# One Trainium2 core: O normalised one head group at a time instead of two, with a new table of exp tiles

## The chip, the cores and the metric

The kernel runs on one core of one Trainium2 chip. The metric is the device time of one execution in microseconds (us). Before the change it was measured three times: 797.41, 797.54 and 798.36 us, median 797.54. One of these executions, of 797.54 us, was recorded by the profiler; every duration below is from that one.

## The reference, cut to what matters

A transformer layer whose two branches start from the same normalised input: multi-query attention (32 query heads of 16 columns, one shared K and one shared V) and a GELU feed-forward, with x (2048 x 512) added.

```python
xn = _layernorm(x)
q = (xn @ wq).reshape(B, S, 32, 16).transpose(0, 2, 1, 3)
k, v = xn @ wk, xn @ wv                       # one K and one V of 16 columns
p = softmax(einsum("bhqd,bkd->bhqk", q, k) * 16 ** -0.5)
o = einsum("bhqk,bkd->bhqd", p, v)
return x + o.transpose(0, 2, 1, 3).reshape(B, S, 512) @ wo + gelu(xn @ w1 + b1) @ w2 + b2
```

## The kernel before, in words

**Tiles and units.** The 2048 queries are cut into 4 blocks of 512 (`NTB`, `TBW`), the 32 heads into 8 groups of 4 (`NGR`, `HG`), so there are 32 (block, group) pairs, numbered `gg`. For each, the scores of 4 heads against 16 tiles of 128 keys make 64 score tiles of 128 keys x 512 queries, 2048 in all. Three consecutive tiles are one unit `u`; 683 units (`NU`) run one after another. A unit is three score matmuls (L851) into three of the eight PSUM banks. Units alternate between banks 0 to 2 and 3 to 5, so the scores of unit u+2 need unit u's banks read out.

**Who takes the exponential.** The string `DTAB` (L51) has one character for each unit. A dot: ScalarE takes all three tiles in one activation of 128x1536 (L870). A digit, 0 or 2: that tile of the unit goes to VectorE and ScalarE takes the other two in one activation of 128x1024. A VectorE tile, called a D tile here, is the sum of five scaled bf16 patterns: one read of PSUM (L887), then, for up to three D tiles together (`KB`), four further additions on the stored integers (L902). A batch is also closed at the last D tile of a group. A D tile costs five value matmuls (L891) instead of one. ScalarE's results stand in a ring of `NE` = 25 buffers `E` of 512 columns until TensorE has read them.

**Normalising O.** The value matmuls of one group add up in bank `pO`: four heads, 32 rows each, of which 16 are O and row 16 is the sum of the exponentials. When a group is complete, `o_evac` (L913) copies the bank to `Of` in f32 (L915), collects the four rows of sums in `den` by a DMA, inverts them on VectorE (L919) and writes them to a scratch row in HBM. Four DMAs then bring the group's 16-row pieces of `Of` to `OfP`, where two head groups fill 128 rows without gaps, and four DMAs broadcast the inverted sums to the same rows of `rbP`. After every second group one VectorE multiply of 128x512 (L937) turns both into `oTp` in bf16, which is the operand of the output projection (`wo_mm`, L1021). Group 30 has no partner and is multiplied in 64 rows; group 31, the last, goes through `o_norm_last` (L940), with its sums transposed by TensorE, no DMA, and a projection of its own (L1168).

**The rest.** Layer norm, its transposes, K and V come first. Q of later groups (`q_pack`, L968), the feed-forward (`h_mm`, `h_chain`, `y_mm`) and the output tiles of the block before (`out_tile`, L1036) are side work with a due unit each (`at`, `q_at`, L1065). An output tile adds the feed-forward, the four pairs of the attention output and the bias in bank 7 (`pM`), which all side matmuls share.

**What sets the order.** The kernel writes down every operation with the data it reads and writes; `Prog.schedule` (L192) then plays the program through with an assumed duration for each operation and fixes from it one order for each engine, `Prog.emit` the semaphore waits. At run time each engine works through its list in order. For a DMA the plan assumes 0.7 us of issue and 2.2 us to landing (L573); all the DMAs of this change are issued on SyncE's queue. When TensorE would be idle, the plan puts matmuls on zeros in between (L1184).

Of the kernel before, what the change touches and what calls it, by code (L numbers as in the profile page):

```python
# [6 lines left out]
ACT = mybir.ActivationFunctionType  # L7
ALU = mybir.AluOpType
AX = mybir.AxisListType

P = 128
# [24 lines left out]
EV_ALLOW = -2.0  # L36
S_WAIT = 0.1
P_WAIT = 0.0
NE_ND_KB = (25, 8, 3)
LA = 34  # L40
LB = 105
LY = 9
# [5 lines left out]
LCO = 0.0  # L48
PRO_FROM = 2.0
TBL = 1  # L50
DTAB = "...00.20.0022.00.2...202202.22..0.200220..220..0.02.222002.20...2200220.2.0.2220.0...200000..002002.2.00..200220..00.200.0000....02.220.22.0220.02...2.22200022.0.2..220..20200220.20.20.220....22.200.2222.020020...2220.222.0222.0.020......2.2..0..020202....0220.20..0022.02.0...22..2220.2020.22.20...0.020020002...0020...02.00..0002202.022....222.2222.2222.0000..222.0.0222.022.200....00000.2020.00.02.2...22202.2.22.0000.000...2.2200.22..22.20.0...2.2.2.002..020020....220.2200.002.22.000....000020.2200.22200...02202.2.2002..2022...222220..0.2222.0020..22.00002.02.222020....20222...0202..0..2...220....2000.2.0.22....2.2.2.00..2.002020...0.00.2202.02000.00...20022.02.00.202000...."  # L51
Y_ALLOW = 8.0
H_ALLOW = 5.0
YT_ALLOW = (3,3,3,3)
# [372 lines left out]
def bass_parallel_sum__grouped_kv_mqa__dense_activation_gelu__prompt_kernel(  # L427
# [18 lines left out]
    H, Dh = 32, 16  # L446
# [3 lines left out]
    TBW = 512  # L450
    NTB = S // TBW
    HG = 4
    NGR = H // HG
    NE, ND, KB = NE_ND_KB
    NPR = 5
    NV = 1 + len(SPL_K)
    KZ = SPL_K.index(0)
    GAM = 128.0 / LN2 * 0.25
    bf, f32 = dt.bfloat16, dt.float32
    i16, i32 = dt.int16, dt.int32  # L460

    with ExitStack() as es:
        def sb(shape, dtype, name):
            return es.enter_context(nc.sbuf_tensor(name, shape, dtype))
# [11 lines left out]
        wop = sb([P, NGR // 2, D], bf, "wop")  # L476
        wol = sb([P, D], bf, "wol")
# [13 lines left out]
        selL = sb([P, 4], f32, "selL")  # L491
# [31 lines left out]
        Dt = sb([P, len(SPL_K), ND, TBW], i16, "Dt")  # L523
        Of = sb([P, 2, TBW], f32, "Of")
        den = sb([P, 2, 16], f32, "den")
        OfP = sb([P, 2, TBW], f32, "OfP")
        rbP = sb([P, 2, TBW], f32, "rbP")
        rX = rbP[:, 0, :].rearrange("p (i r) -> p i r", i=4)
        rd_dram = nc.dram_tensor("rden_rows", [NTB * NGR, HG * TBW], f32).ap()
        oT = sb([P, TBW], bf, "oT")  # L530
        oTp = sb([P, NPR, TBW], bf, "oTp")

        pAll = es.enter_context(nc.psum_tensor("pAll", [P, 8 * 512], f32))

        def bank(b, n=1):
            return pAll[:, b * 512:(b + n) * 512]
# [6 lines left out]
        def B(b):  # L543
            return ("bank", b)
# [4 lines left out]
        def dve(fn, r=(), w=(), n=TBW, mode=1, allow=1.0, **kw):  # L549
            return add("dve", fn, r, w, occ=vcost(n, mode), lat=0.16, allow=allow, **kw)  # L550

        def act(fn, r=(), w=(), n=TBW, allow=0.0, **kw):
            return add("act", fn, r, w, occ=0.051 + n / 1.2e3, lat=0.22, allow=allow, **kw)

        def mm(o, l, rh, start, stop, r=(), w=(), tp=None, skip=False, occ=0.216, allow=1.5, **ak):
            kw = {}
            if tp is not None:
                kw["tile_position"] = tp
            if skip:
                kw["skip_group_check"] = True  # L560
            return add("pe", lambda e: e.matmul(o, l, rh, start=start, stop=stop, **kw), r, w, occ=occ, lat=0.23,  # L561
                       allow=allow, **ak)
# [10 lines left out]
        def dma(eng, o, i, stream, r=(), w=(), lat=2.2, allow=1.0, **kw):  # L573
            return add(eng, lambda e: e.dma_start(o, i), r, w, dma=stream, occ=0.7, lat=lat, allow=allow, **kw)
# [13 lines left out]
        def setup(fn, r=(), w=(), occ=0.25, due=0.0, **kw):  # L588
            return add("pool", fn, r, w, occ=occ, lat=0.15, due=due, **kw)
# [188 lines left out]
        for _, _, kind, a in sorted(steps, key=lambda s: s[:2]):  # L778
# [17 lines left out]
            due=0.0)  # L796
# [116 lines left out]
        def o_evac(gg):  # L913
            i = gg % 2
            dve(lambda e: e.tensor_copy(Of[:, i, :], pO), w=["O", ("Of", i)], allow=0.0)  # L915
            row = Of[16:17, i, :]
            dma("sp", den[:, i, :], bass.AP(row.tensor, row.offset, [[32 * row.ap[0][0], HG], [1, TBW]]),
                f"d_den{i}", r=[("Of", i)], w=[("den", i)])
            dve(lambda e: e.reciprocal(den[:, i, :], den[:, i, :]), r=[("den", i)], w=[("den", i)], n=120)  # L919
            dma("sp", rd_dram[gg:gg + 1, :], den[:, i, :], f"d_rd{i}", r=[("den", i)], w=[("rd", i)])  # L920
            pp, h = divmod(gg, 2)
            s, sl = pp % 2, pp % NPR
            for j in range(HG):
                r0 = 64 * h + Dh * j
                dma("sp", OfP[r0:r0 + Dh, s, :], Of[32 * j:32 * j + Dh, i, :], f"d_of{s}{h}{j}", r=[("Of", i)], w=[("OfP", s, h, j)])
            for j in range(HG):
                r0 = 64 * h + Dh * j
                src = rd_dram[gg:gg + 1, j * TBW:(j + 1) * TBW]
                dma("sp", rbP[r0:r0 + Dh, s, :], bass.AP(src.tensor, src.offset, [[0, Dh], [1, TBW]]), f"d_rb{s}{h}{j}",
                    r=[("rd", i)], w=[("rbP", s, h, j)])  # L930
            end = gg == NTB * NGR - 2
            if end:
                setup(lambda e: e.memset(oTp[64:P, sl, :], 0.0), w=[("oTp", sl)], occ=0.4)
            if h or end:
                n = 64 if end else P
                keys = [(k, s, hh, j) for k in ("OfP", "rbP") for hh in range(h + 1) for j in range(HG)]
                onorm[gg - h] = onorm[gg] = dve(lambda e: e.tensor_tensor(oTp[0:n, sl, :], OfP[0:n, s, :], rbP[0:n, s, :], ALU.mult),  # L937
                                                r=keys, w=[("oTp", sl)], allow=3.0)

        def o_norm_last(gg):  # L940
            RB1 = [[("rbP", 0, h, j) for j in range(HG)] for h in range(2)]
            for h in range(2):
                c = slice(h * 256, h * 256 + 256)
                dve(lambda e, c=c: e.tensor_copy(Of[:, 1, c], pO[:, c]), w=["O", ("Of", 1), ("Of", 2 + h)], n=256, due=0.0)
            for h in range(2):
                for i in (2 * h, 2 * h + 1):
                    mm(bank(h)[:, 4 * i:4 * i + 4], Of[:, 1, i * P:(i + 1) * P], selL[:], True, True,
                       r=[("Of", 2 + h), "selL"], w=[B(h)], occ=0.2, due=0.0)
            for h in range(2):
                dve(lambda e, h=h: e.reciprocal(rT[:, 2 * h:2 * h + 2, :],  # L950
                                                bank(h)[:, 8 * h:8 * h + 8].rearrange("p (i j) -> p i j", j=4)),
                    w=[B(h), ("rT", h)], n=100, due=0.0)
                o = rX[:, 2 * h:2 * h + 2, :].rearrange("p i (j r) -> p i j r", j=4)
                i_ = rT[:, 2 * h:2 * h + 2, :].unsqueeze(3).to_broadcast([P, 2, 4, 32])
                if h == 0:
                    dve(lambda e, o=o, i_=i_: e.tensor_copy(o, i_), r=[("rT", h)], w=[("rX", h)] + RB1[h], n=256, due=0.0)
                else:
                    act(lambda e, o=o, i_=i_: e.activation(o, i_, ACT.Copy), r=[("rT", h)], w=[("rX", h)] + RB1[h], n=256, due=0.0)
            for h in range(2):
                for i in (2 * h, 2 * h + 1):  # L960
                    add("pe", lambda e, i=i, h=h: e.transpose(bank(h)[:, 128 + (i % 2) * P:256 + (i % 2) * P], rX[:, i, :], ident_f[:]),
                        r=[("rX", h), "ident_f"], w=[B(h)], occ=0.15, lat=0.22, due=0.0)
            for h in range(2):
                c = slice(h * 256, h * 256 + 256)
                dve(lambda e, h=h, c=c: e.tensor_tensor(oT[:, c], Of[:, 1, c], bank(h)[:, 128:384], ALU.mult),
                    r=[("Of", 2 + h)], w=[B(h), ("oTl", 0) if h == 0 else ("oTl", 1)], n=256, due=0.0)

        def q_pack(tb, p, gls=(0, 1)):  # L968
            s = p % 2
# [51 lines left out]
        def wo_mm(tb, i, ps, start=False, bk=7, al=1.5):  # L1021
            for n, p in enumerate(ps):
                pp = tb * NGR // 2 + p
                hs = [h for h in range(2) if 2 * pp + h < NTB * NGR - 1]
                assert all(2 * pp + h in onorm for h in hs)
                mm4(bank(bk), oTp[:, pp % NPR, i * P:(i + 1) * P], wop[:, p, :], start and n == 0, False,
                   r=[("oTp", pp % NPR), "wop"], w=[B(bk)], allow=al)

        def b2_mm(bk=7, stop=True, al=1.5):
            mm4(bank(bk), ones, b2row[:], False, stop, r=["ones", "b2row"], w=[B(bk)], allow=al)  # L1030
# [134 lines left out]
        for i in range(4):  # L1165
            wo_mm(tb, i, range(FIN_G, NGR // 2), start=i < 3, bk=FB[i], al=WF_ALLOW)
        for i in range(4):
            mm4(bank(FB[i]), oT[:, i * P:(i + 1) * P], wol[:, :], False, True,  # L1168
               r=[("oTl", i // 2), "wol"], w=[B(FB[i])], due=0.0)
        for i in (0, 1, 3, 2):  # L1170
            ti = tb * 4 + i
            w = [(B(FB[i]), j) for j in range(4)] + ([B(FB[i])] if i < 3 else []) + [("x", ti)]
# [50 lines left out]
```

## Time and profile before

| | |
|---|---|
| time of the profiled execution | 797.54 us |
| its span, first to last instruction | 795.8 us |
| median of three runs | 797.54 us |
| ScalarE (ACT) busy | 774.0 us, 97% |
| TensorE (PE) busy, the zero matmuls among it | 767.0 us, 96% |
| VectorE (DVE) busy | 739.8 us, 93% |
| first exp starts, last exp ends | 30.0 us, 786.6 us |
| D tiles, and exps over three tiles | 439, 243 |

Span and time of the profiled execution differ by 1.7 us, which lie outside the recorded instructions. Busy time is the time in which at least one instruction of the engine runs; successive instructions of one engine overlap at their edges, so that a mean duration times the count comes out above it. The chain of waits follows the work that ended last back from the end, at each step to the instruction that released it, and its pieces do not overlap. "A <- B" in the table of waits says that A stood idle until B ended.

### The profile page before, as it was taken

How to read it: one execution, taken by the hardware profiler on the slowest of the kernel's cores; microseconds unless marked ns; L12 is line 12 of the kernel's file. 1: busy time of each engine (PE TensorE's matmuls, PEld its weight loads, DVE VectorE, ACT ScalarE, POOL GpSimd, SP SyncE). 2: the span in 40 equal slices, each digit the busy share in tenths (PEclk: the TensorE clock that was granted, in tenths of full speed). 3: DMA queues.
4: the chain of work that ended last, by engine and by line, in shares of the span. 5: the costliest groups of instructions: out<-in, count | busy, mean ns of one | idle time of the engine just before them, and what ended most of it. 6: DMA issues, size and time to landing. Idle time of an engine off the chain costs nothing.

```text
span 795.8 us, 20778 instructions
## 1 busy us (share of the span) xinstructions
PE 767.0 (96%) x8759; PEld 240.5 (30%) x8759; DVE 739.8 (93%) x1401; ACT 774.0 (97%) x734; POOL 20.8 (3%) x84
## 2 busy tenths in 40 slices
PE   6799999999999999999999999999999999999998
PEld 4323322232222323322232233322233233323222
DVE  8589999999998959999999889999999998999896
ACT  4899999999999999999999999999999999999995
POOL 6300000000000000000000000000000000000000
PEclk7899999999999999999999999999999999999999
DMA  9101100000000010001000001100001010000001
GB/s 312 41 9 30 23 15 16 17 21 13 12 22 23 23 29 16 17 15 22 17 13 24 20 19 23 22 16 16 19 12 22 24 22 23 16 9 16 16 9 35
DMA packets 30007, 21.17 MB, mean 27 GB/s; under 512 B 16353, under 2 KB 25434, under 8 KB 29914
## 3 DMA queue, kind: packets, MB, share of 16 engines
q1 hardware_dynamic: 28330, 19.28, 9.4%
q8 instruction: 69, 1.13, 0.6%
q10 hardware_dynamic: 1584, 0.56, 0.3%
q14 instruction: 24, 0.20, 0.1%
HBM read 10.98 MB, written 2.35 MB: 17 GB/s over the span
## 4 chain that ended last, share of the span: by engine, by line
ACT 92%; PE 5%; DVE 3%; DMA 0%; issue 0%; DVEq 0%
ACT E L870 88%; ACT ub L1012 3%; PE pAll L891 2%; PE pAll L851 1%; DVE stats L660 1%; PE pAll L567 1%; PE pAll L561 1%; DVE Dt L887 0%; DVE Dt L902 0%; DMA x_sb<-in_A_x_dram 0%; ACT xnT L718 0%; PE pAll L713 0%; ACT KT L732 0%; ACT ub L700 0%; DVE ub L697 0%
## 5 line engine op out<-in xcount | busy, mean ns | idle before, releaser
L870 ACT ACTIVATE E<-pAll 128x1024 bf16<-128x1024 f32 (+1 forms) x683 | 736.7, 1335 | 1.5 <-PE pAll L851 1.3
L891 PE MATMUL pAll<-Dt,V 128*32 128x512 bf16 x2195 | 390.0, 383 | 0.3
L887 DVE TENSOR_SCALAR Dt<-pAll 128x512 int16<-128x512 f32 x439 | 292.9, 680 | 28.9 <-PE pAll L851 28.3
L891 PE MATMUL pAll<-E,V 128*32 128x512 bf16 x1609 | 303.2, 387 | 1.4 <-DVE Of L915 1.2
L902 DVE TENSOR_SCALAR Dt<-Dt 128x1536 int16<-128x1536 int16 (+1 forms) x608 | 297.6, 533 | 0.9
L851 PE MATMUL pAll<-QT,KT 32*128 32x512 bf16 x2048 | 268.3, 386 | 15.0 <-ACT E L870 8.4
L851 PEld LDWEIGHTS pAll<-QT,KT 32*128 32x128 bf16 x2048 | 68.8, 91 | 290.4 <-ACT E L870 222.9
L891 PEld LDWEIGHTS pAll<-Dt,V 128*32 128x32 bf16 x2195 | 105.6, 94 | 107.0 <-issue 54.8
L567 PE MATMUL pAll<-xnT,w_sb 128*32 128x512 bf16 x896 | 128.1, 382 | 0.1
L567 PE MATMUL pAll<-w_sb,ub 128*32 128x512 bf16 x896 | 125.4, 382 | 0.0
L891 PEld LDWEIGHTS pAll<-E,V 128*32 128x32 bf16 x1609 | 70.7, 93 | 77.0 <-issue 59.1
L567 PE MATMUL pAll<-wop,oTp 128*32 128x512 bf16 x256 | 50.8, 381 | 0.0
L998 DVE TENSOR_SCALAR hb<-pAll,b1T 128x512 bf16<-128x512 f32 x56 | 41.5, 740 | 0.8 <-PE pAll L891 0.5
L567 PEld LDWEIGHTS pAll<-xnT,w_sb 128*32 128x32 bf16 x896 | 33.6, 95 | 24.1 <-issue 10.0
L567 PEld LDWEIGHTS pAll<-w_sb,ub 128*32 128x32 bf16 x896 | 32.1, 95 | 11.8 <-issue 5.2
L1184 PE MATMUL pAll<-xnT,zeros 128*32 128x512 bf16 x308 | 33.1, 383 | 0.0
L1012 ACT ACTIVATE ub<-ub 128x1536 bf16<-128x1536 bf16 (+1 forms) x20 | 32.1, 1606 | 0.0
L915 DVE COPY Of<-pAll 128x512 f32<-128x512 f32 x31 | 21.1, 680 | 5.0 <-PE pAll L567 4.1
L567 PE MATMUL pAll<-xnT,wq_sb 128*32 128x512 bf16 x256 | 20.5, 398 | 0.0
L1011 DVE TENSOR_TENSOR ub<-ub,hb 128x1536 bf16<-128x1536 bf16 (+1 forms) x20 | 17.9, 893 | 0.1
L1014 DVE TENSOR_TENSOR ub<-ub,hb 128x1536 bf16<-128x1536 bf16 (+1 forms) x20 | 17.9, 894 | 0.1
L1009 DVE TENSOR_TENSOR ub<-hb 128x1536 bf16<-128x1536 bf16 (+1 forms) x20 | 17.8, 892 | 0.1
(124 smaller groups left out, 242.7 us busy)
## 6 DMA issues: line engine op xcount, KB each, us to landing
OfP<-Of SPq DMA_DIRECT2D x124, 32.0 KB, 1.9
rbP<-rden_rows SPq DMA_DIRECT2D x124, 32.0 KB, 1.8
w_sb<-in_B_w_dram SPq DMA_DIRECT2D x2, 1792.0 KB, 13.5
x_sb<-in_A_x_dram SPq DMA_DIRECT2D x8, 256.0 KB, 6.1
out_dram<-x_sb SPq DMA_DIRECT2D x16, 128.0 KB, 1.7
QT<-qp SPq DMA_DIRECT2D x124, 16.0 KB, 1.8
wq_sb<-in_A_wq_dram ACTq DMA_DIRECT2D x1, 512.0 KB, 6.5
wop<-in_A_wo_dram SPq DMA_DIRECT2D x1, 512.0 KB, 16.3
```

The source lines that it names most:

```text
L567: add("pe", lambda e, c=c, j=j: e.matmul(o[c, :], l[:, c], rh, start=start, stop=stop, tile_position=(0, 32 * j)), r, [(k, j) for k in w] ...
L851: ins = e.matmul(o, l, rh, start=True, stop=True, tile_position=(q0, 0))
L870: exps.append(act(lambda e: e.activation(E[:, s0:s0 + na, :], bank(b0, na).rearrange("p (a n) -> p a n", a=na), ACT.Exp, scale=LN2 / 128.0 ...
L887: dve(lambda e: e.tensor_scalar(Dt[:, KZ, s, :], bank(bk), float(127 * 128) + SPL_D, SPL_MIN, ALU.add, ALU.max), w=[B(bk), ("D", s, KZ)], ...
L891: add("pe", lambda e, a, b: e.matmul(pO[32 * j:32 * j + 32, :], V1[:, v, kt, :], rhs, start=a, stop=b, tile_position=(0, 32 * j)), r=r + [ ...
L902: dve(lambda e, k=k: e.tensor_scalar(Dt[:, k, s0:s0 + n, :], Dt[:, KZ, s0:s0 + n, :], float(SPL_K[k]), None, ALU.add), r=[("D", s0 + i, KZ ...
L915: dve(lambda e: e.tensor_copy(Of[:, i, :], pO), w=["O", ("Of", i)], allow=0.0)
L998: dve(lambda e: e.tensor_scalar(hb[:, ft % 6, :], pM, b1T[:, ft:ft + 1], None, ALU.add), r=["b1T"], w=M4 + [("h", ft % 6)], allow=ev)
L1011: dve(lambda e: e.tensor_tensor(uu, uu, hh, ALU.mult), r=uk + hk, w=uk, n=c, mode=2, allow=al)
L1012: act(lambda e: e.activation(uu, uu, ACT.Tanh, scale=GELU_K), r=uk, w=uk, n=c, allow=al - 0.5, kind="tanh")
L1014: dve(lambda e: e.tensor_tensor(uu, uu, hh, ALU.mult), r=uk + hk, w=uk, n=c, mode=2, allow=al)
L1184: pr.filler = lambda e, j, o: e.matmul((pO if o else pM)[32 * j:32 * j + 32, :], zeros[:, 0:32], xnT[:, 0, 0:TBW], start=not o, stop=not o ...
```

## The change

Two things of the loop are changed, and one size. First, O is normalised for each group by itself. The four broadcasts now fill `rbc` in the padded layout of `Of` (32 rows a head), one multiply for each group writes bf16 to `oT` (three buffers, `NOT`), and four DMAs bring its 16-row pieces to `oTp`. The multiply runs for groups 0 to 30; before, there was one for each of 15 pairs and one for group 30. The copies of `Of` to `OfP` are gone. Second, the table `DTAB` is another one: 429 of its 683 characters are digits instead of 439. In groups 0 to 7, 8 to 15, 16 to 23 and 24 to 31 there are 109, 109, 111 and 100 D tiles, where there were 111, 109, 112 and 107. Third, `NE` is 24 instead of 25. The last group's tail reads `Of`'s other buffer; the projection of Q, `q_pack`, is the same in both kernels.

```diff
-NE_ND_KB = (25, 8, 3)
+NE_ND_KB = (24, 8, 3)
...
-DTAB = "...00.20.0022.00.2...202202.22..0.200220..220..0.02.222002.20...2200220.2.0.2220.0...200000..002002.2.00..200220..00.200.0000....02.220.22.0220.02...2.22200022.0.2..220..20200220.20.20.220....22.200.2222.020020...2220.222.0222.0.020......2.2..0..020202....0220.20..0022.02.0...22..2220.2020.22.20...0.020020002...0020...02.00..0002202.022....222.2222.2222.0000..222.0.0222.022.200....00000.2020.00.02.2...22202.2.22.0000.000...2.2200.22..22.20.0...2.2.2.002..020020....220.2200.002.22.000....000020.2200.22200...02202.2.2002..2022...222220..0.2222.0020..22.00002.02.222020....20222...0202..0..2...220....2000.2.0.22....2.2.2.00..2.002020...0.00.2202.02000.00...20022.02.00.202000...."
+DTAB = "...00.002.0.22.002...220220.222..00.2020...00..002..0200.0220...02222.0.2.02.02220...2.0000..000002.0.20..2.002.0..2000.02000...222.200202.02..020...2.2.2000.20000.2.20..2000020.022.2.2200.....22200.2222..20020...2220.222.0222.000.0..22..2.2.02.2.00.02....2220..2.0002220..2.....2.22.02002.20.020..22.000.2.2000..2020....2200200.0.2002.22...20.222022.22..22200..222.202.2020.2.200....20020.202000.0.00....22222.2202.202.2000...0.022.20202...020.....220...22.02.02002....22022020.00..0020...2.000..22022220.2.0...022..022200.2.2022...222220.20.2222..020..2.220002.02.222.2.....20.......202.2.........2.20.222..222.22...22.2..0.0..2.020020...02.0.22.2002202.02...22002.02.0020.2000...."
...
-    NPR = 5
+    NOT, NPR = 3, 5
...
         den = sb([P, 2, 16], f32, "den")
-        OfP = sb([P, 2, TBW], f32, "OfP")
-        rbP = sb([P, 2, TBW], f32, "rbP")
-        rX = rbP[:, 0, :].rearrange("p (i r) -> p i r", i=4)
+        rbc = sb([P, 2, TBW], f32, "rbc")
+        rX = rbc[:, 1, :].rearrange("p (i r) -> p i r", i=4)
         rd_dram = nc.dram_tensor("rden_rows", [NTB * NGR, HG * TBW], f32).ap()
-        oT = sb([P, TBW], bf, "oT")
+        oT = sb([P, NOT, TBW], bf, "oT")
         oTp = sb([P, NPR, TBW], bf, "oTp")
...
                 f"d_den{i}", r=[("Of", i)], w=[("den", i)])
             dve(lambda e: e.reciprocal(den[:, i, :], den[:, i, :]), r=[("den", i)], w=[("den", i)], n=120)
             dma("sp", rd_dram[gg:gg + 1, :], den[:, i, :], f"d_rd{i}", r=[("den", i)], w=[("rd", i)])
+            for j in range(HG):
+                src = rd_dram[gg:gg + 1, j * TBW:(j + 1) * TBW]
+                dma("sp", rbc[32 * j:32 * j + 32, i, :], bass.AP(src.tensor, src.offset, [[0, 32], [1, TBW]]),
+                    f"d_rb{i}{j}", r=[("rd", i)], w=[("rbc", i, j)])
+            tb, g = divmod(gg, NGR)
+            onorm[gg] = dve(lambda e: e.tensor_tensor(oT[:, gg % NOT, :], Of[:, i, :], rbc[:, i, :], ALU.mult),
+                            r=[("Of", i)] + [("rbc", i, j) for j in range(HG)], w=[("oT", gg % NOT)], allow=3.0)
             pp, h = divmod(gg, 2)
-            s, sl = pp % 2, pp % NPR
+            if gg == NTB * NGR - 2:
+                setup(lambda e: e.memset(oTp[64:P, pp % NPR, :], 0.0), w=[("oTp", pp % NPR, 1, j) for j in range(HG)], occ=0.4)
             for j in range(HG):
                 r0 = 64 * h + Dh * j
-                dma("sp", OfP[r0:r0 + Dh, s, :], Of[32 * j:32 * j + Dh, i, :], f"d_of{s}{h}{j}", r=[("Of", i)], w=[("OfP", s, h, j)])
-            for j in range(HG):
-                r0 = 64 * h + Dh * j
-                src = rd_dram[gg:gg + 1, j * TBW:(j + 1) * TBW]
-                dma("sp", rbP[r0:r0 + Dh, s, :], bass.AP(src.tensor, src.offset, [[0, Dh], [1, TBW]]), f"d_rb{s}{h}{j}",
-                    r=[("rd", i)], w=[("rbP", s, h, j)])
-            end = gg == NTB * NGR - 2
-            if end:
-                setup(lambda e: e.memset(oTp[64:P, sl, :], 0.0), w=[("oTp", sl)], occ=0.4)
-            if h or end:
-                n = 64 if end else P
-                keys = [(k, s, hh, j) for k in ("OfP", "rbP") for hh in range(h + 1) for j in range(HG)]
-                onorm[gg - h] = onorm[gg] = dve(lambda e: e.tensor_tensor(oTp[0:n, sl, :], OfP[0:n, s, :], rbP[0:n, s, :], ALU.mult),
-                                                r=keys, w=[("oTp", sl)], allow=3.0)
+                dma("sp", oTp[r0:r0 + Dh, pp % NPR, :], oT[32 * j:32 * j + Dh, gg % NOT, :], f"d_op{gg % NOT}{j}",
+                    r=[("oT", gg % NOT)], w=[("oTp", pp % NPR, h, j)])
 
         def o_norm_last(gg):
-            RB1 = [[("rbP", 0, h, j) for j in range(HG)] for h in range(2)]
+            RB1 = [("rbc", 1, j) for j in range(HG)]
             for h in range(2):
                 c = slice(h * 256, h * 256 + 256)
-                dve(lambda e, c=c: e.tensor_copy(Of[:, 1, c], pO[:, c]), w=["O", ("Of", 1), ("Of", 2 + h)], n=256, due=0.0)
+                dve(lambda e, c=c: e.tensor_copy(Of[:, 0, c], pO[:, c]), w=["O", ("Of", 2 * h)], n=256, due=0.0)
...
-                    mm(bank(h)[:, 4 * i:4 * i + 4], Of[:, 1, i * P:(i + 1) * P], selL[:], True, True,
-                       r=[("Of", 2 + h), "selL"], w=[B(h)], occ=0.2, due=0.0)
+                    mm(bank(h)[:, 4 * i:4 * i + 4], Of[:, 0, i * P:(i + 1) * P], selL[:], True, True,
+                       r=[("Of", 2 * h), "selL"], w=[B(h)], occ=0.2, due=0.0)
...
-                    dve(lambda e, o=o, i_=i_: e.tensor_copy(o, i_), r=[("rT", h)], w=[("rX", h)] + RB1[h], n=256, due=0.0)
+                    dve(lambda e, o=o, i_=i_: e.tensor_copy(o, i_), r=[("rT", h)], w=[("rX", h)] + RB1, n=256, due=0.0)
                 else:
-                    act(lambda e, o=o, i_=i_: e.activation(o, i_, ACT.Copy), r=[("rT", h)], w=[("rX", h)] + RB1[h], n=256, due=0.0)
+                    act(lambda e, o=o, i_=i_: e.activation(o, i_, ACT.Copy), r=[("rT", h)], w=[("rX", h)] + RB1, n=256, due=0.0)
...
-                dve(lambda e, h=h, c=c: e.tensor_tensor(oT[:, c], Of[:, 1, c], bank(h)[:, 128:384], ALU.mult),
-                    r=[("Of", 2 + h)], w=[B(h), ("oTl", 0) if h == 0 else ("oTl", 1)], n=256, due=0.0)
+                dve(lambda e, h=h, c=c: e.tensor_tensor(oT[:, gg % NOT, c], Of[:, 0, c], bank(h)[:, 128:384], ALU.mult),
+                    r=[("Of", 2 * h)], w=[B(h), ("oT", gg % NOT) if h == 0 else ("oTl", 1)], n=256, due=0.0)
...
                 mm4(bank(bk), oTp[:, pp % NPR, i * P:(i + 1) * P], wop[:, p, :], start and n == 0, False,
-                   r=[("oTp", pp % NPR), "wop"], w=[B(bk)], allow=al)
+                   r=[("oTp", pp % NPR, h, j) for h in range(2) for j in range(HG)] + ["wop"], w=[B(bk)], allow=al)
...
         for i in range(4):
-            mm4(bank(FB[i]), oT[:, i * P:(i + 1) * P], wol[:, :], False, True,
-               r=[("oTl", i // 2), "wol"], w=[B(FB[i])], due=0.0)
+            mm4(bank(FB[i]), oT[:, (NTB * NGR - 1) % NOT, i * P:(i + 1) * P], wol[:, :], False, True,
+               r=[("oT", (NTB * NGR - 1) % NOT) if i < 2 else ("oTl", 1), "wol"], w=[B(FB[i])], due=0.0)
```

## The prediction

> **What bounds the kernel now.** I read the chain of waits first, by engine and line, then ScalarE's own waits.
>
> ```profile
> ACT 92%; PE 5%; DVE 3%; DMA 0%; issue 0%; DVEq 0%
> ```
>
> ```profile
> ACT E L870 <- PE pAll L851: 1.3, 2, 0.7
> ```
>
> ScalarE carries 92% of the chain. The line of the waits (total, times, longest) is the only wait of an exp on another engine: 1.3 us for 683 exps. Busy time by stretch says the same for each stage (columns: length, then PE, PEld, DVE, ACT busy, each with its count):
>
> ```profile
> 60.00:230.00 170.00, 165.69 (x1778) 49.92 (x1775) 168.70 (x322) 170.00 (x161) 0.00 (x0) 1.00 0.08 19
> 230.00:430.00 200.00, 197.37 (x2291) 60.45 (x2291) 186.86 (x353) 200.00 (x186) 0.00 (x0) 1.00 0.08 19
> 430.00:630.00 200.00, 196.35 (x2294) 59.75 (x2287) 190.44 (x357) 199.40 (x188) 0.00 (x0) 1.00 0.08 20
> ```
>
> ScalarE never stands still in the first two, and for 0.6 us in the third. TensorE and VectorE are nearly as full, but both have gaps, and ScalarE has none: from 30.0 us (first exp) to 786.6 us (end of the last) the time is ScalarE's work and nothing else. In front of it lie 30.0 us of layer norm, behind it 9.2 us of tail, around the span 1.7 us.
>
> **The change part by part.**
>
> *ScalarE: ten tiles more.* The table has 429 D tiles instead of 439, so ten exps grow from two tiles to three. What a tile costs must be read from the chain, since successive exps overlap and their mean durations contain the overlap:
>
> ```profile
> 691.43 1.36 ACT ub L1012
> 692.79 6.78 ACT E L870 x6
> ...
> 718.54 3.18 ACT E L870 x3
> ...
> 729.86 0.94 ACT ub L1012
> ```
>
> The two tanh pieces (start, length) are 1536 and 1024 columns wide: 512 columns cost 1.36 - 0.94 = 0.42 us. With 0.92 us for an exp of two tiles and 1.34 for three, three exps with one wide one make 2 x 0.92 + 1.34 = 3.18, and six with three wide ones 3 x 0.92 + 3 x 1.34 = 6.78: both pieces come out exactly. The longest undisturbed pieces agree (in 87.98 us stand 52 narrow and 30 wide exps: 52 x 0.92 + 30 x 1.34 = 88.0). So the ten tiles cost 10 x 0.42 = **+4.2 us** on the engine that sets the time, and ScalarE has no gap to put them in.
>
> *VectorE: ten D tiles less, fifteen multiplies more.*
>
> ```profile
> L887 DVE TENSOR_SCALAR Dt<-pAll 128x512 int16<-128x512 f32 x439 | 292.9, 680 | 28.9 <-PE pAll L851 28.3
> L902 DVE TENSOR_SCALAR Dt<-Dt 128x1536 int16<-128x1536 int16 x548 | 277.4, 548 | 0.9
> L937 DVE TENSOR_TENSOR oTp<-OfP,rbP 128x512 bf16<-128x512 f32 x15 | 10.2, 682 | 0.1
> ```
>
> Ten reads of PSUM fall away: 10 x 0.680 = 6.8 us. Batching the new table by threes and at group ends gives 130 batches of three, 17 of two and 5 of one, where there were 137, 13 and 2; with four additions each at 548, 415 and 279 ns (the rows of the three widths) that is 5.3 us less. Added are 31 multiplies for 16: 15 x 0.682 = 10.2 us. The sum is -1.9 us, spread unevenly. By blocks I get +0.3, +3.3, +2.1 and -7.6 us. The first is the delicate one: there VectorE is busy 168.7 of 170 us. Blocks two and three have about 13 and 10 us of gaps. VectorE's work is hidden behind ScalarE's as long as each D tile's scores are read in time: an exp of two tiles lasts 0.92 us, and TensorE needs 0.39 us to refill the banks, so a read may come about half a microsecond late. A multiply in front of it holds it up by at most 0.60 us (the step from one such instruction to the next in the chain, L1052 at 766.0). Bounds for what the 15 extra multiplies cost: below nothing, if the 1.5 us that the exps stood idle in all vanish with the ten D tiles; at most 15 x 0.60 = 9.0 us, if each is passed on whole. I take 0: 31 copies of `Of` and 16 multiplies of the same size stand in the same list now, and all exps together waited 1.5 us.
>
> [...]
>
> *TensorE.* Ten D tiles less are 10 x 5 value matmuls less and 10 more of the plain kind: 40 less. Fifteen matmuls of this width take 0.87 us, four side by side (the chain at 787.1), so 2.3 us fall away, on an engine that fills its gaps with zero matmuls. I cost this at nothing; were TensorE the bound it would be a gain of 2.3.
>
> *DMAs.* For each group ten are issued on SP before and after: one of sums, one of inverses, four broadcasts, four pieces. What moves is their place. The four pieces were issued at once behind `Of`, beside the inversion. Now they come behind the multiply, and the broadcasts are twice as large.
>
> ```profile
> OfP<-Of SPq DMA_DIRECT2D x124, 32.0 KB, 1.9
> rbP<-rden_rows SPq DMA_DIRECT2D x124, 32.0 KB, 1.8
> ...
> QT<-qp SPq DMA_DIRECT2D x124, 16.0 KB, 1.8
> ```
>
> The new pieces are 16 rows of 1 KB, like those of `qp`: eight of these issue in 4.95 us, 0.62 each, and land in 1.8. The hop lengthens the path from `Of` to the projection by 4 x 0.62 + 1.8 = 4.3 us. The broadcasts of 64 KB have no row; between a 32 KB one (1.8) and x's 256 KB (6.1) I take 2 us, near the first. On SP what queues behind a waiting piece is the next group's `den`, Q's pieces and the output stores. A multiply comes 18 to 20 us after its `Of` (82.1 to 100.2; 219.1 to 238.3), groups are some 24 us apart and scores never waited for a Q piece, so I cost this at nothing. It surfaces where the last pair of a block is needed at once: the first output tile of the second block is made at the start of the third and needs a pair whose multiply ran at 429.67; TensorE used it at 430.0. Now that is some 4.3 us later, three times, in bank 7, behind which only side work queues. The plan's own allowance for the hop, 4 x 0.7 + 2.2 = 5.0 us, is more than 4.3, so TensorE's list should hold other work until the data are there.
>
> *E ring.* 24 buffers instead of 25 are 24 / (1609/683 = 2.36 a unit) = 10 units instead of 10.6 of lead. No exp waited for a value matmul, so 0; half a microsecond of slack is gone.
>
> *Tail.* Group 30's multiply ran at 783.1. The hop puts its `oTp` at 783.8 + 4.3 = 788.1, after the last exp. Sixteen matmuls need it, 0.87 us. Of the tail's 9.2 us TensorE spends 788.9 to 789.6 on such matmuls anyway while it waits for the inverted sums. Bounds: 0 if they all fit, 0.9 if none does; I take **+0.3**, nearer to the gap that is there. The second buffer of `Of` costs nothing: the multiply at 783.1 is 4 us ahead of the copy at 787.2 that overwrites it.
>
> *Sum.* 797.54 + 4.2 + 0.3 = **802.0 us**. The profiled execution equals the median of the runs, so nothing is to be shifted. A measurement of this kernel can tell about 0.2% (1.6 us) from no change; this is +0.56%.
>
> **The rivals.**
>
> *VectorE becomes the bound in the first block.* For it: 168.7 of 170 us, and a net +0.3. Against it: the 1.3 us of gaps there still cover 0.3. If the four extra multiplies there each hold up an exp whole, 4 x 0.60 = 2.4 us are added: 804.4 us. Chance 0.09.
>
> *The late pair stops TensorE.* If the hop overruns the plan at the three block boundaries, TensorE waits at the head of its list, scores queue behind it, and ScalarE has one unit (1.1 us) in hand: up to 4.3 - 1.1 = 3.2 each, 9.6 in all, 811.6 us. For it: broadcasts landed up to 3.4 us after issue instead of 1.8. Against it: the plan's 5.0 us and a multiply that VectorE's own queue, not the DMA, sets. Chance 0.04.
>
> *Faster: the tail gives back more than the exps cost.* One mechanism: group 30's matmuls leave the way of the last group's. In the tail VectorE waits for TensorE 2.4 + 0.5 + 1.2 = 4.1 us, 2.4 of it before the copy of `Of`. Faster than before needs 4.2 and more from there, all that TensorE costs the tail; with the exps' idle 1.5 us gained as well it would be 797.54 + 4.2 - 4.1 - 1.5 = 796.1 us. Against it: most of the 2.4 us is the wait for the last exp's own value matmuls, which stay. Chance 0.02; that it gives back about half to all of the 4.2 and the time stays within 0.2%, 0.03.
>
> *The change does not do what its name says.* Projecting Q, `q_pack`, is untouched, so nothing is to be gained or lost there; this gives the forecast.
>
> **How the numbers follow.** Forecast 0.82, rivals 0.09, 0.04, 0.02 and 0.03. The range reaches down to 802.0 - 0.3 - 1.5 = 800.2 (tail at nothing, idle time gone) and up to the first rival with a dearer tail, 801.7 + 2.4 + 0.9 = 805.0. The bound of 9.0 us and the second rival are left out, with the faster side: about 1 in 10. Faster by over 0.2%: 0.02; within: 0.03; slower: 0.95.
>
> **What would show it.** Right: 253 exps of 128x1536 and 430 of 128x1024, ScalarE again at 170.0 and 200.0 in the stretches of the middle, its last exp ending near 790.8, and 31 multiplies with little idle time before them. The hop: pieces of 16 KB landing in about 1.8 us. Wrong: exps that wait for L851 by more than 2 us in all, above all between 60 and 230 us (first rival) or right after 215, 409 and 600 (second), or a tail that is not 9.2 to 10.1 us long. If 512 columns more did not cost 0.42 us, the main term falls.

## The result

The changed kernel takes 802.55 us (median of four runs, 802.16 to 802.83), the kernel before on the same chip 797.95: a ratio of 1.0057 with a 95% interval of 1.0039 to 1.0074 (intervals below are of the same kind). The profiled execution took 802.16 us with a span of 800.4; before, 797.54 and 795.8. So 4.6 us are to be found.

From the page of the changed kernel, the chain of waits by engine; it is to be read against the 92% for ScalarE before.

```profile
ACT 75%; PE 17%; DVE 6%; DMA 1%; issue 0%; ACTq 0%; DVEq 0%; POOL 0%
```

This looks as if TensorE had taken over. It has not. Busy time by stretch (length, then PE, PEld, DVE, ACT) shows ScalarE as full as before:

```profile
60.00:230.00 170.00, 166.79 (x1800) 49.15 (x1801) 168.24 (x321) 170.00 (x160) 0.00 (x0) 1.00 0.08 21
230.00:430.00 200.00, 197.35 (x2252) 60.78 (x2246) 189.15 (x361) 199.72 (x186) 0.00 (x0) 1.00 0.09 22
430.00:630.00 200.00, 195.97 (x2225) 59.52 (x2221) 191.85 (x364) 199.41 (x187) 0.00 (x0) 1.00 0.08 21
630.00:760.00 130.00, 126.89 (x1584) 38.96 (x1585) 111.63 (x204) 130.00 (x117) 0.52 (x1) 1.00 0.08 21
```

The chain follows the last releaser back, and between 500 and 557 us and from 736.6 us on it runs along TensorE and VectorE, while ScalarE beside them is idle for 0.6 of 111.7 us. Scores and exps are so closely interlocked that the chain can take either side. An engine that is busy 130.00 of 130 us has no slack of its own; that it sets the pace is what the experiments below test. The groups of ScalarE and VectorE, by form (busy us, mean ns, idle before):

```profile
L869 ACT ACTIVATE E<-pAll 128x1024 bf16<-128x1024 f32 x430 | 439.4, 1195 | 0.7 <-PE pAll L850 0.6
L869 ACT ACTIVATE E<-pAll 128x1536 bf16<-128x1536 f32 x253 | 378.6, 1615 | 1.0 <-PE pAll L850 0.9
...
L886 DVE TENSOR_SCALAR Dt<-pAll 128x512 int16<-128x512 f32 x429 | 287.5, 681 | 33.5 <-PE pAll L850 32.2
L901 DVE TENSOR_SCALAR Dt<-Dt 128x1536 int16<-128x1536 int16 x520 | 264.0, 548 | 0.9
...
L925 DVE TENSOR_TENSOR oT<-Of,rbc 128x512 bf16<-128x512 f32 x31 | 21.1, 681 | 0.0
```

Ten exps are wider, ten D tiles gone, and 31 multiplies stand where there were 16, without idle time before them.

**A budget of ScalarE.** Successive exps overlap by about a quarter of a microsecond (1195 and 1615 ns are their mean durations), so an exp can come that much late without any idle time showing. The ends of successive exps do not have this fault. In both traces an exp of two tiles ends 0.917 us after its predecessor and one of three 1.343 us after it (nine in ten of the steps are at most 2 ns longer). Counting these steps, tanhs of the same widths included, gives ScalarE's work; what the stretch from the first exp's start to the last one's end is longer is lateness, which I split at 45 us. (In both kernels 0.11 us of the first part is the first exp's own longer duration, and 0.4 us of the second part are the 20 tanhs, which take 0.02 us more than exps of their width.) With the start and the tail the span is complete:

| us | before | changed | difference |
|---|---|---|---|
| first exp starts | 30.00 | 28.92 | -1.08 |
| ScalarE's work | 754.99 | 759.25 | +4.26 |
| late, up to 45 us | 0.53 | 1.42 | +0.89 |
| late, after 45 us | 1.12 | 1.53 | +0.41 |
| tail after the last exp | 9.18 | 9.32 | +0.14 |
| span | 795.8 | 800.4 | +4.6 |

### The profile page after: what moved, and what is told of

Read it like the earlier page. It is cut to its first block, busy times and chain, and to the rows that moved or that the text cites. A ratio compares the mean times of both kernels' runs of the same rounds, so it can differ in the third digit from the quotient of the medians.

```text
span 800.4 us, 20727 instructions
## 1 busy us (share of the span) xinstructions
PE 770.0 (96%) x8735; PEld 240.6 (30%) x8735; DVE 738.2 (92%) x1406; ACT 778.4 (97%) x734; POOL 20.3 (3%) x84
## 4 chain that ended last, share of the span: by engine, by line
ACT 75%; PE 17%; DVE 6%; DMA 1%; issue 0%; ACTq 0%; DVEq 0%; POOL 0%
ACT E L869 71%; PE pAll L890 7%; PE pAll L850 5%; PE pAll L566 4%; ACT ub L1007 3%; DVE Dt L886 2%; DVE Dt L901 1%; DVE hb L993 1%; DMA wq_sb<-in_A_wq_dram 1%; PE pAll L560 1%; ACT ub L699 1%; ACT xnT L717 0%; DVE ub L1004 0%; DVE ub L1006 0%; DVE ub L1009 0%
## 5 line engine op out<-in xcount | busy, mean ns | idle before, releaser
L890 PE MATMUL pAll<-Dt,V 128*32 128x512 bf16 x2145 | 382.1, 383 | 0.5
L886 DVE TENSOR_SCALAR Dt<-pAll 128x512 int16<-128x512 f32 x429 | 287.5, 681 | 33.5 <-PE pAll L850 32.2
L901 DVE TENSOR_SCALAR Dt<-Dt 128x1536 int16<-128x1536 int16 (+2 forms) x608 | 292.3, 525 | 0.9
L890 PEld LDWEIGHTS pAll<-Dt,V 128*32 128x32 bf16 x2145 | 103.3, 94 | 108.6 <-issue 56.7
L566 PE MATMUL pAll<-xnT,w_sb 128*32 128x512 bf16 x896 | 115.1, 382 | 1.3 <-DVE hb L993 0.9
L566 PE MATMUL pAll<-wop,oTp 128*32 128x512 bf16 x256 | 47.7, 381 | 0.0
L566 PEld LDWEIGHTS pAll<-xnT,w_sb 128*32 128x32 bf16 x896 | 30.7, 95 | 23.3 <-issue 8.6
L925 DVE TENSOR_TENSOR oT<-Of,rbc 128x512 bf16<-128x512 f32 x31 | 21.1, 681 | 0.0
L1009 DVE TENSOR_TENSOR ub<-ub,hb 128x1536 bf16<-128x1536 bf16 (+1 forms) x20 | 17.9, 894 | 0.1
```

The source lines that it names most:

```text
L566: add("pe", lambda e, c=c, j=j: e.matmul(o[c, :], l[:, c], rh, start=start, stop=stop, tile_position=(0, 32 * j)), r, [(k, j) for k in w] ...
L886: dve(lambda e: e.tensor_scalar(Dt[:, KZ, s, :], bank(bk), float(127 * 128) + SPL_D, SPL_MIN, ALU.add, ALU.max), w=[B(bk), ("D", s, KZ)], ...
L890: add("pe", lambda e, a, b: e.matmul(pO[32 * j:32 * j + 32, :], V1[:, v, kt, :], rhs, start=a, stop=b, tile_position=(0, 32 * j)), r=r + [ ...
L901: dve(lambda e, k=k: e.tensor_scalar(Dt[:, k, s0:s0 + n, :], Dt[:, KZ, s0:s0 + n, :], float(SPL_K[k]), None, ALU.add), r=[("D", s0 + i, KZ ...
L925: onorm[gg] = dve(lambda e: e.tensor_tensor(oT[:, gg % NOT, :], Of[:, i, :], rbc[:, i, :], ALU.mult), r=[("Of", i)] + [("rbc", i, j) for j ...
```

## The experiments

The theory: ten more tiles on ScalarE are the loss, and the other way of normalising O is hidden. The rival: the O path (fifteen more multiplies, a later DMA hop) is the loss. All ratios are to the kernel before, on the same chip.

**Ten tiles more, nothing else.** The kernel before, with its lists as they are; `MORE` names ten units with a D tile, spread over the loop:

```diff
-            exps.append(act(lambda e: e.activation(E[:, s0:s0 + na, :], ...
+            exps.append(act(lambda e: ((e.activation(scr[:], bank(b0), ACT.Exp, scale=LN2 / 128.0) if u in MORE else None),
+                                       e.activation(E[:, s0:s0 + na, :], ...)[1],
```

> The kernel before, every engine's list as it is, but in ten units that have a D tile, spread over the loop, ScalarE takes an extra exp of 512 columns into a tile that nobody reads: ten tiles more for ScalarE, nothing less for VectorE and nothing changed in the normalising of O. Theory (ten tiles more on ScalarE are the loss): 10 x 0.43 = 4.3 us, or up to 5 with the fixed part of a separate instruction, more than 797.8: 802.1 to 802.8 us, the changed kernel's time without its O path. Rival (ScalarE has room, the O path is the loss): 797.8 us.

Measured: 802.51 us, ratio 1.0056 (1.0041 to 1.0071), before 798.25: +4.26. ScalarE's exps in this run, by form:

```profile
L871 ACT ACTIVATE E<-pAll 128x1024 bf16<-128x1024 f32 x440 | 450.2, 1192 | 1.2 <-PE pAll L852 1.0
L871 ACT ACTIVATE E<-pAll 128x1536 bf16<-128x1536 f32 x243 | 365.2, 1604 | 0.7 <-PE pAll L852 0.7
...
L871 ACT ACTIVATE scr<-pAll 128x512 bf16<-128x512 f32 x10 | 7.7, 766 | 0.0
```

The ten added steps are 0.490 us each in the trace, 4.9 in all. The span grew by 4.5, since the first exp started 0.84 us earlier than in the profile of before and the exps up to 45 us came 0.54 us later. Everything of the old O path is still there, and the time is that of the changed kernel: ScalarE had no room.

**Ten, and sixty, tiles less.** The changed kernel, lists as they are, with the last tile of ten or sixty wide exps (`CUT`) left out:

```diff
+            nx = na - 1 if u in CUT else na
-            exps.append(act(lambda e: e.activation(E[:, s0:s0 + na, :], bank(b0, na).rearrange("p (a n) -> p a n", a=na),
+            exps.append(act(lambda e: e.activation(E[:, s0:s0 + nx, :], bank(b0, nx).rearrange("p (a n) -> p a n", a=nx),
```

> The changed kernel with every engine's list as it is, but ten of its three-tile exps, spread evenly over the loop, work on 1024 columns instead of 1536: the third tile's exponentials are left out and stale ones are read in their place, so this part of the softmax is not computed. Theory (the ten tiles given to ScalarE are the whole loss): 10 x 0.42 = 4.2 us less than the changed kernel's 802.55, 798.3 us, within 0.6. Rival (the fifteen added multiplies and the DMA hop are the loss, the tiles are hidden): 802.5 us, unchanged.

> The changed kernel with every engine's list as it is, but sixty of its three-tile exps, spread evenly, work on 1024 columns: the third tile's exponentials are left out and stale ones read in their place. ScalarE has 60 x 0.426 = 25.6 us less. Theory (ScalarE's tiles set the time only as far as the other lists have room): ten narrowed exps gave 4.3 on ScalarE but made other exps late by 0.8; for sixty the other engines should take back half or more: 785 to 792 us. Rival (ScalarE alone is the bound): 777 us.

Ten: 799.59 us (798.34 to 801.28), ratio 1.0026 (1.0016 to 1.0037), 3 us less than the changed kernel: above the theory's range, far from the rival. Its profile has 754.99 us of ScalarE's work, but 3.05 us of lateness after 45 us instead of 1.53 (1.5 more, not the 0.8 that the second expectation gives). Sixty, a single execution: 797.72 us, outside what theory and rival had said. Of 25.6 us less work 18.4 came back as lateness after 45 us (19.9 instead of 1.5; 89 exps late by over 0.05 us), although no other engine got more to do. A row by stretch and the exps' wait in that run:

```profile
430.00:630.00 200.00, 197.30 (x2248) 61.20 (x2245) 192.88 (x368) 196.34 (x190) 0.00 (x0) 1.00 0.08 22
```

```profile
ACT E L871 <- PE pAll L851: 7.9, 29, 1.0
```

So ScalarE sets the time upwards, tile for tile. Downwards the other lists, planned for ScalarE's old pace, take over after a handful of tiles: the late exps wait for their scores, and in this stretch TensorE is the fuller engine. Whether TensorE's own work or VectorE's late reads hold the scores up was not separated.

**The multiplies, shorter and doubled.** The changed kernel, lists as they are:

```diff
 # shorter
-e.tensor_tensor(oT[:, gg % NOT, :], Of[:, i, :], rbc[:, i, :], ALU.mult)
+e.tensor_tensor(oT[:, gg % NOT, 0:512 if gg < NOT else 64], Of[:, i, 0:512 if gg < NOT else 64], ...
 # doubled
+(e.tensor_tensor(scr[:], Of[:, i, :], rbc[:, i, :], ALU.mult), e.tensor_tensor(oT[:, gg % NOT, :], ...))[1]
```

> The changed kernel with every engine's list as it is, but 28 of the 31 multiplies of O (groups 3 to 30) work on 64 of their 512 columns: the other columns of O are not normalised. VectorE has about 28 x 0.45 = 12.6 us less to do (0.68 us for a multiply; 0.24 us for the inversion of 16 columns is the nearest short row). Theory (VectorE's added multiplies are hidden behind ScalarE): unchanged, 802.5 us, at best 0.9 us less, which is what the exps and tanhs now stand idle in the middle of the loop. Rival (the multiplies hold up exps): up to 12.6 us less, 790 us; by half 796.

> The changed kernel with every engine's list as it is, but each of the 31 multiplies of O is done twice in a row (the first time into an unused tile): 31 x 0.60 = 18.6 us more on VectorE. Theory (hidden as long as VectorE has gaps): in the first block its gaps of 1.8 us cannot cover 8 x 0.60 = 4.8, so up to 3 us there, nothing in the others, whose gaps are 8 us and more: 802.6 to 805.6 us. Rival (a multiply in front of a D tile's read holds up an exp): all of it, 821 us.

Shorter: 803.03 us, ratio 1.0067 (1.0055 to 1.0080). Nothing is won. VectorE is busy 10.1 us less (728.1 instead of 738.2), and 6.7 us of that turn into waiting for scores; from the table of waits (total, times, longest; 32.2 us in the changed kernel):

```profile
DVE Dt L886 <- PE pAll L850: 38.9, 41, 4.3
```

Doubled: 810.07 us, ratio 1.0156 (1.0142 to 1.0170), 7.5 us more than the changed kernel. That lies between theory and rival, and refutes my reading by stretches. I had let gaps of 8 us and more cover the later blocks; the busy times and the waits of this run:

```profile
60.00:230.00 170.00, 165.42 (x1770) 49.39 (x1769) 169.24 (x322) 168.77 (x159) 0.00 (x0) 1.00 0.08 20
230.00:430.00 200.00, 195.50 (x2217) 60.37 (x2209) 191.24 (x365) 198.37 (x184) 0.00 (x0) 1.00 0.08 22
430.00:630.00 200.00, 194.03 (x2211) 59.86 (x2208) 194.55 (x369) 198.36 (x185) 0.00 (x0) 1.00 0.08 22
```

```profile
ACT E L869 <- PE pAll L850: 4.6, 15, 0.7
```

VectorE still has 9 and 5 us of gaps in the later two stretches, and ScalarE falls behind in all three. By the steps the exps are 9.8 us late after 45 us instead of 1.5: 2.2, 3.2 and 2.8 us in these stretches, in small pieces, some of them a few microseconds after a multiply. One such place, from VectorE's and ScalarE's timeline:

```profile
217.29 0.69 DVE L925 TENSOR_TENSOR scr<-Of,rbc 128x512 bf16<-128x512 f32 x1
217.89 0.69 DVE L925 TENSOR_TENSOR oT<-Of,rbc 128x512 bf16<-128x512 f32 x1
```

```profile
220.41 4.71 ACT L869 ACTIVATE E<-pAll 128x1024 bf16<-128x1024 f32 x5 [0.22 <-PE pAll L850]
```

The gaps are only in part where the multiplies stand. On average 0.6 us more on VectorE made the exps 0.27 us later (8.2 us for 31). The pair also shows the step of 0.60 us between two operations of 0.69 that I had used.

**The ring.** `NE_ND_KB = (25, 8, 3)` in the changed kernel.

> The changed kernel with 25 buffers E instead of 24, all else the same. Theory (ScalarE never waits for a buffer): 802.5 us, unchanged. Rival (the smaller ring holds up exps at group ends): 0.5 us for each group end that it held up, up to 2 us less, 800.5 us.

803.17 us (801.69 to 804.20), ratio 1.0064 (1.0049 to 1.0079): no gain. After 45 us its exps are late by 1.53 us, as with 24.

**Tables.** Four runs put another table into one of the kernels, which is then planned anew. The edits are the string `DTAB`: that of before in the changed kernel, that of the change in the kernel before, ten digits of its own turned to dots in the kernel before, and the last quarter of the table of before in the changed kernel.

> The changed kernel with the table of before (439 D tiles), planned anew. ScalarE has ten tiles less, 4.2 us; VectorE has 12.1 us more than in the changed kernel. Theory (the ten tiles were the price of the fifteen multiplies: VectorE's list has no room for both): twice the multiplies, 18.6 us more on VectorE, made exps late by 8 us, so 12.1 us more should make them late by about 5: 802.5 - 4.2 + 5.2 = 803.5 us or more. Rival (VectorE has room and the table was merely chosen too small): 798.3 us.

> The kernel before with the table of the change (429 D tiles), planned anew: O is still normalised for two groups at once, VectorE has 12.1 us less to do than before. Theory (ScalarE's tiles alone set the time wherever VectorE and TensorE keep up): 797.8 + 4.2 = 802.0 us. Rival (a table suits the kernel for which it was fitted, since it fixes where in the loop VectorE and TensorE are full): later than that by several us, 805 or more.

> The kernel before with ten digits of its own table, evenly spread over the loop, turned into dots (429 D tiles), planned anew. ScalarE has 4.3 us more, VectorE 12 less. Theory (ScalarE's tiles alone, as in the run with ten extra exps at unchanged lists): 797.9 + 4.3 = 802.2 us. Rival (every new table orders all lists anew, and an order that was not fitted costs by itself, even with less work for VectorE): 804 us or more, the excess as exps that wait for L851.

> The changed kernel with the table of before in the last quarter of the units (from unit 512 on), 436 D tiles, planned anew: seven of the ten tiles go back to VectorE where its gaps are widest (18 us between 630 and 760 us). Theory (the tiles were given up there for the tail: the side work of the last block then lies behind in VectorE's and TensorE's lists): the last exp ends about 3 us earlier than in the changed kernel, but the tail of 9.3 us grows by more, 804 us or later. Rival (there was room): 802.5 - 3.0 = 799.5 us.

| | D tiles | time, us | ratio (interval) | work | late after 45 | tail |
|---|---|---|---|---|---|---|
| changed, table of before | 439 | 817.45 | 1.0244 (1.0227 to 1.0261) | 754.99 | 10.7 | 19.3 |
| before, table of the change | 429 | 807.52 | 1.0125 (1.0108 to 1.0142) | 759.25 | 5.1 | 10.0 |
| before, ten digits less | 429 | 804.47 | 1.0086 (1.0071 to 1.0102) | 759.25 | 1.9 | 10.3 |
| changed, old last quarter | 436 | 808.49 | 1.0135 (1.0119 to 1.0150) | 756.26 | 2.2 | 17.3 |

None beats its own kernel, not even those that take work from VectorE. Work follows the count to the digit; the rest is mainly lateness and tail, which I put down to the order of the lists, though no run changes the order alone. In the second run another part shows: 0.8 of its 5.1 us fall in and just behind a stretch from 391.5 to 398.3 us in which TensorE's granted clock was 0.50. The rivals' times held for the second and third run (805 or more, 804 or more). In the first and last the theory's bounds held (803.5 or more, 804 or later), but were passed by 14 and 4.5 us, a size that no expectation had. With ten digits less the excess over 802.2 us is 2.3 us, about half of it a longer tail and not late exps, as the rival had put it. The last run shows one way in which a table with more D tiles is not simply better. Its last exp ended at 789.3 us, 1.8 earlier than in the changed kernel (expected: 3), and then TensorE (timeline) still had feed-forward to do, and ScalarE's last copy waited for it:

```profile
795.03 2.33 PE L566 MATMUL pAll<-w_sb,ub 128*32 128x512 bf16 x40
...
798.88 3.21 PE L566 MATMUL pAll<-w_sb,ub 128*32 128x512 bf16 x56 [0.88 <-DVE x_sb L1047]
```

```profile
803.73 0.60 ACT L1172 ACTIVATE x_sb<-pAll 128x512 bf16<-128x512 f32 x1 [11.01 <-PE pAll L566]
```

In the changed kernel that copy waited 2.2 us; with the whole old table it waited 13.5.

**The start.** The kernel before with `FILL_FROM = 26.0`.

> The kernel before with the zero matmuls allowed four microseconds earlier in the plan (FILL_FROM 26 instead of 30), all else the same. TensorE's granted clock stood at 0.50 from about 29 to 35 us in the kernel before and to 39 us in the changed one, and the exps up to 45 us were late by 0.4 and 1.3 us in all. Theory (zero matmuls between the first scores end the slow stretch sooner): 0.3 to 0.9 us less than before. Rival (the clock's stretches are set by the idle time ahead of the first scores): unchanged, 797.9 us.

798.24 us, ratio 1.0009 (0.9998 to 1.0019): nothing won. TensorE's slow stretch did end earlier, at 34.1 us, but the exps up to 45 us were 1.4 us late, not 0.5 as before. The profiled execution was the slowest of eleven, 800.37 us. In it the exps between 60 and 230 us were 1.8 us late, almost all of it at two exps, in and just behind a second slow stretch from 157.0 to 160.4 us (by stretch, then ScalarE's timeline):

```profile
156.96:160.37 3.41, 3.41 (x34) 0.98 (x33) 3.08 (x7) 2.71 (x3) 0.00 (x0) 0.50 0.06 14
```

```profile
159.42 1.02 ACT L870 ACTIVATE E<-pAll 128x1024 bf16<-128x1024 f32 x1 [0.70 <-PE pAll L851]
```

## Why the prediction was right, point by point

*Ten tiles on ScalarE, +4.2.* Right: 0.426 us a tile by the steps, 4.26 in all, and the run that added only them (as exps of their own, 4.9 us of work) took the changed kernel's time within the spread of the runs.

*VectorE, -1.9, spread +0.3, +3.3, +2.1 and -7.6.* Busy time fell by 1.6 us (739.8 to 738.2). By stretch it changed by -0.5, +2.3, +1.4 and, between 630 and 760 us, -10.5: the pattern holds.

*The multiplies cost the exps nothing.* Right in size: 0.4 us more lateness after 45 us, and 28 of the multiplies shortened brought nothing back. But the reason was only half right. I had argued from gaps; the doubled multiplies show that the gaps cover only a part, 10.4 of 18.6 us. That the multiplies cost nothing in the changed kernel is most likely because its lists were laid out with them, which no run shows by itself. The outer bound of 9.0 us for fifteen was too far (4.0 at 0.27 each), yet 0 is not a property of a multiply.

*DMAs, nothing.* Right. Broadcasts of 64 KB landed in 2.1 us (taken: 2), pieces in 1.8; four issued in 2.4 us, so the hop is 4.2 (taken: 4.3). From the page:

```profile
rbc<-rden_rows SPq DMA_DIRECT2D x124, 64.0 KB, 2.1
...
oTp<-oT SPq DMA_DIRECT2D x124, 16.0 KB, 1.8
```

The hop surfaces where it was expected, but larger than the 4.3 us: the first output tiles of the three blocks, added at 242.22, 432.06 and 619.21 us before, are added at 247.36, 441.85 and 628.76, 5 to 10 us later. At the second of them 2.0 us are the pair's multiply itself (429.67, then 431.71); where the rest comes from was not traced. VectorE stood idle before none of the three. Its waits for output tiles grew elsewhere (L1041 before: 3.9 us in all, longest 2.5); the longest now lies before the tile added at 676.06:

```profile
DVE x_sb L1036 <- PE pAll L566: 6.6, 4, 5.7
```

No exp was late for it: after 45 us only two exps and a tanh were late by over 0.05 us; they ended at 278, 328 and 559 us, none of them at a block's start, so the second rival falls. (One reading was too narrow: the multiplies of before ran 13 to 24 us after the second group's copy, not 18 to 20.) The first falls too, with 0.1 us of lateness between 60 and 230 us.

*Tail, +0.3.* +0.14. Group 30's multiply came at 786.99, its pieces were issued until 790.97, and the matmuls left of the projection ran at 793.1, 794.0 and 795.2, in gaps in which TensorE waits for the last group; VectorE, SyncE and TensorE in the timeline:

```profile
786.99 0.69 DVE L925 TENSOR_TENSOR oT<-Of,rbc 128x512 bf16<-128x512 f32 x1
...
787.70 3.27 SPq L573 DMA_DIRECT2D oTp<-oT  x4
...
793.11 0.62 PE L566 MATMUL pAll<-wop,oTp 128*32 128x512 bf16 x8
```

*What the sum left out.* The start: the first exp came 1.08 us earlier and the next ones 0.89 us later. The two nearly cancel, and neither was in the sum: that it came within 0.6 us is in part luck. And the prediction took the ten tiles as given. Why the table gives them up stays partly open: with the old table the changed kernel is 15 us slower still, and its old last quarter, with seven tiles more, 6 us, but a table with 439 D tiles fitted to the changed kernel was not tried, nor was the hop taken away by itself.

## What to carry to other kernels

Where one engine runs without gaps, price a change by the steps between the ends of its successive instructions; durations contained overlap here (1195 ns for an exp whose step is 917), and idle time did not show lateness that was shorter than this overlap of about 0.28 us. Adding to that engine cost nearly all of it here (4.26 us for 4.9 us of exps); taking from it paid only until the next list was late, which was a handful of tiles (3.0 us for ten, 4.8 for sixty). Gaps in another engine's busy time need not lie at the place where new work must stand (of 18.6 us more on VectorE 8.2 reached the exps), and a table of assignments that suits one kernel can be a poor one in another whose lists differ.

## What the runs showed of the hardware

*ScalarE was very regular.* A step of an exp from PSUM took 0.490, 0.917 and 1.343 us for 512, 1024 and 1536 columns: 0.426 for each 512, and 0.064 that did not grow with the width. Of the steps of the two wider ones nine in ten were at most 2 ns longer. The tanhs from SBUF, 0.935 and 1.362 us for 1024 and 1536 columns, have the same slope.

*TensorE's granted clock fell to 0.50 just as the loop began, for 3.4, 6.8 or 10.2 us.* The granted clock stood at 0.50 from 28.3 to 35.1 us in the kernel before and from 28.8 to 39.1 in the changed one. Two rows by stretch, of the kernel before and of the changed one (the granted clock is the third number from the end):

```profile
36.00:38.00 2.00, 1.46 (x17) 0.34 (x13) 1.56 (x4) 2.00 (x3) 0.00 (x0) 1.00 0.10 26
```

```profile
36.00:38.00 2.00, 2.00 (x16) 0.37 (x13) 1.71 (x4) 1.59 (x3) 0.00 (x0) 0.50 0.10 25
```

In thirteen profiles the slow stretch lasted 3.4 us once, 6.8 twice and 10.2 ten times, and the first exp started between 28.9 and 30.7 us. In two of them the clock also fell to 0.50 in the middle of the loop: in the run with `FILL_FROM = 26.0` from 157.0 to 160.4 us, in the kernel before with the table of the change from 391.5 to 398.3. What starts and ends these stretches was not shown, nor how much of the spread between executions (801.69 to 804.20 us for one kernel) they make. Of the eleven executions with `FILL_FROM = 26.0` the three with a mean granted clock of 0.991 took 799.54 to 800.37 us and the eight with 0.993 to 0.996 took 797.16 to 798.64, but the four of the changed kernel show no such order.
